# Moving one parameter row, its exponential and the early loads in an S5 + MLP kernel

## The chip, the cores and the metric

One core of one Trainium2 chip. The metric is the device time of one execution in microseconds (us); the medians below are over the timed executions. An execution counts as slow when it is over 1.5% above the fastest of its kernel. All but the slow ones named below had a granted TensorE clock of 1.00 (0.998 and above), with one exception that is also named. One timed execution of each kernel is also the profiled one, from which the lines come; its span, from the first to the last instruction, is nearly 2 us shorter than its time. Spans are compared with spans and timed medians with timed medians.

## The reference, cut to what matters

Two branches read the same 2048 tokens of 640 features; a sigmoid of a dot product mixes them.

```python
# A: a diagonal complex state space model, 640 states
dt      = exp(log_dt)
Lam_bar = exp(dt * (Lambda_re + 1j * Lambda_im))   # |Lam_bar| = exp(dt*Lambda_re) = r_c in the kernel
B_bar   = ((Lam_bar - 1) / Lam)[:, None] * Bmat
h_t     = Lam_bar * h_{t-1} + x_t @ B_bar          # 2048 steps
a       = 2 * real(h @ C) + x * Dskip
# B: an MLP, 640 -> 1728 -> 640
b       = gelu(x @ w1 + b1) @ w2 + b2
out     = g * a + (1 - g) * b,   g = sigmoid(x . gate_w)
```

The kernel turns the complex recurrence into two real scans with the constant factor `r_c`, on inputs rotated by tables of cosine and sine (`TCOS`, `TSIN`). The modulus `r_c` is needed at the first scan; its angle, dt times `Lambda_im`, is needed for the tables.

## The kernel before: the parts concerned

The tokens are handled in four chunks of 512. TensorE, VectorE and ScalarE follow a hand-written order. The early loads go out on two queues, SyncE's and ScalarE's, in the order of this code:

```python
load_x0(nc.sync, 0, 1, 0, KA * P)      # token tile 0, columns 0..255, 64 KB
load_w1a(nc.scalar, 0)                 # slab 0 of w1, 192 KB
load_x0(nc.sync, 1, 2, 0, KA * P)
load_w1a(nc.scalar, 1)
load_x0(nc.sync, 2, 3, 0, KA * P)
load_w1a(nc.scalar, 2)
load_x0(nc.sync, 3, 4, 0, KA * P)
# ... memsets of prmA, prmB ...
nc.scalar.activation(out=warm[:], ..., func=ACT.Exp)        # brings the table in
load_turned(0)                                              # transposed load, columns 256..639
rows(nc.sync,   prmA[2 * KS:3 * KS, :], A_Lambda_re)        # parameter rows, 1.2 KB each
rows(nc.scalar, prmA[0:KS, :], A_log_dt)
rows(nc.scalar, prmA[KS:2 * KS, :], A_Lambda_im)
load_turned(H)
load_w1a(nc.sync, 4)
load_w1a(nc.sync, 3)
# ... w1b slabs; with the second of them the rows of prmB: b1, gate_w ...
```

A row holds one parameter vector as 5 partitions of 128 values. A matmul with an identity turns a tile of rows into columns (`colA`, `colB`), which VectorE and ScalarE can use as scalars:

```python
part(0, 2); part(1, 2); part(0, 3)                          # matmuls of w1 slabs 0 and 1
nc.tensor.matmul(pP[:, 0:3 * KS], lhsT=prmA[:], rhs=ident[:, 0:3 * KS], ...)
nc.vector.tensor_copy(out=colA[:], in_=pP[:, 0:3 * KS])     # log_dt, Lambda_im, Lambda_re
nc.scalar.activation(out=dt16[:], in_=ldt_c, func=ACT.Exp)
# ... limp ...
nc.vector.tensor_tensor(out=dtl[:], in0=dt16[:], in1=lre_c, op=ALU.mult)
nc.vector.tensor_tensor(out=thp_c[:], in0=dt16[:], in1=limp[:], op=ALU.mult)
nc.scalar.activation(out=r_c[:], in_=dtl[:], func=ACT.Exp)
# ... the angles u ...
part(1, 3)
strip(2, 0, HT, False)                                      # first matmuls of w1 slab 2
# ... slabs 2 and 4; the two sines on ScalarE ...
for kf in range(FA):                                        # slab 3
    if kf == 3:
        nc.tensor.matmul(pA[:, 0:NB], lhsT=prmB[:], rhs=ident[:, 0:NB], ...)
        nc.vector.tensor_copy(out=colB[:], in_=pA[:, 0:NB])
# ... GELUs; VectorE widens the sine table by angle doubling ...
nc.vector.tensor_scalar(out=nsH[:], in0=sH, scalar1=-1.0, ...)   # then TCOS, TSIN, then the scans
```

## Time and profile before

| | before |
|---|---|
| time, median of 3 runs, us | 216.03 (215.61 to 216.46) |
| span of the profiled execution, us | 214.29 |
| start of the `colA` copy (VectorE), us | 8.42 |
| start of the `colB` copy (VectorE), us | 12.05 |
| start of the first product of the first scan, us | 28.20 |

The last three rows are the moments by which the start is followed here. The `colA` copy tells when the rows are in, the `colB` copy when VectorE's unbroken work begins, and the first product when the tables are ready. Lines from the queues of ScalarE and SyncE in the timeline (start, length in us, engine, line, operation, output and input):

```profile
0.73 1.39 ACTq L127 DMA_DIRECT2D w1a<-in_B_w_dram  x3
4.04 0.52 ACTq L130 DMA_DIRECT2D prmA<-in_A_log_dt_dram  x1
2.60 1.32 SPq L151 DMA_TRANSPOSE xT<-in_A_x_dram  x1
```

Slab 2 is the third of the first line and goes out at about 1.65. The rows go out only at 4.04, and the first transposed load at 2.60.

### The profile page before, as it was taken

What the parts mean: (1) busy time and instruction counts of PE and PEld (TensorE: products, weight loads), DVE (VectorE), ACT (ScalarE), POOL (GpSimd) and SP (SyncE); (2) the same over time, 40 slices, a digit from 0 to 9 for tenths busy, and PEclk for the clock granted to TensorE, in tenths of its full rate; (3) what the DMA queues carried; (4) which work ended last, traced back from release to release, by engine and by line L of the source; (5) the groups of instructions that cost most, each with busy time, mean ns of one, the idle gap of its engine ahead of it and who ended that gap; (6) DMA issues with size and microseconds to landing.
All of it is one profiled execution on the core that took longest, in us unless ns stands there. A gap on an engine that the chain in (4) does not pass through costs nothing.

```text
span 214.3 us, 3539 instructions
## 1 busy us (share of the span) xinstructions
PE 209.6 (98%) x1383; PEld 125.6 (59%) x1383; DVE 187.9 (88%) x381; ACT 101.7 (47%) x182; POOL 1.9 (1%) x15
## 2 busy tenths in 40 slices
PE   8899999999999999999999999999999999999994
PEld 5745444454576644775457777444457577676773
DVE  2489999999998999998999999899999999995153
ACT  3499856675759579203663210456682421405100
POOL 1001000000000000000000000000000000000000
DMA  6899999999000000051000005100000000110012
GB/s 183 207 177 206 206 202 286 348 195 227 3 0 0 3 0 0 14 173 50 25 0 3 0 0 177 45 26 0 2 5 12 0 3 0 61 64 0 0 63 64
DMA packets 33139, 16.23 MB, mean 76 GB/s; under 512 B 24546, under 2 KB 33122, under 8 KB 33122
## 3 DMA queue, kind: packets, MB, share of 16 engines
q1 hardware_dynamic: 32526, 15.38, 29.9%
q10 hardware_dynamic: 596, 0.63, 0.9%
q8 instruction: 11, 0.18, 0.4%
q14 instruction: 6, 0.05, 0.1%
HBM read 7.48 MB, written 2.62 MB: 47 GB/s over the span
## 4 chain that ended last, share of the span: by engine, by line
DVE 70%; PE 20%; DMA 5%; issue 2%; ACT 1%; ACTq 0%; DVEq 0%
DVE g L497 19%; PE bank L661 10%; DVE wa L478 10%; DVE wb L478 10%; PE bank L602 7%; DVE v L478 6%; DVE hs L478 6%; DMA out_dram<-ot 4%; DVE bank L576 3%; DVE ot L666 3%; PE bank L274 2%; DMA prmA<-in_A_Lambda_im_dram 2%; DVE CT_re L466 2%; DVE CT_im L466 2%; DVE g L426 1%
## 5 line engine op out<-in xcount | busy, mean ns | idle before, releaser
L602 PE MATMUL bank<-w_sb,gel 128*128 128x384 bf16 (+1 forms) x416 | 57.9, 299 | 0.0
L602 PEld LDWEIGHTS <-gel 128*128 128x128 bf16 x416 | 40.3, 98 | 17.0 <-issue 0.8
L546 ACT ACTIVATE bu<-bank 128x512 bf16<-128x512 f32 x40 | 23.6, 597 | 37.3 <-PE bank L543 37.2
L661 PEld LDWEIGHTS <-hs 128*128 128x128 bf16 x330 | 31.7, 98 | 12.1 <-issue 0.4
L279 ACT ACTIVATE gel<-bank,colB 128x512 bf16<-128x512 f32 x52 | 33.7, 694 | 10.6 <-PE bank L274 10.3
L497 DVE TENSOR_TENSOR_SCAN g<-r_c,carry,v 128x512 bf16<-128x512 f32 x30 | 37.2, 1270 | 0.0
L610 ACT ACTIVATE gb<-bank,gcol 128x384 f32<-128x384 f32 (+1 forms) x32 | 15.1, 526 | 31.7 <-PE bank L602 16.5
L274 PE MATMUL bank<-xT,w1a 128*128 128x512 bf16 (+2 forms) x162 | 27.7, 328 | 0.0
L666 DVE SCALAR_TENSOR_TENSOR ot<-bank,gcol,gb 128x320 bf16<-128x320 f32 (+2 forms) x33 | 17.5, 532 | 11.5 <-PE bank L661 9.5
L661 PE MATMUL bank<-CT_re,hs 128*128 128x320 bf16 (+2 forms) x165 | 27.1, 295 | 0.2 <-DVE bank L576 0.2
L661 PE MATMUL bank<-CT_im,hs 128*128 128x320 bf16 (+2 forms) x165 | 27.1, 295 | 0.0
L543 PE MATMUL bank<-xT,BT_re 128*128 128x512 bf16 x100 | 24.9, 379 | 0.0
L543 PE MATMUL bank<-xT,BT_im 128*128 128x512 bf16 x100 | 24.8, 379 | 0.0
L274 PEld LDWEIGHTS <-w1a 128*128 128x128 bf16 x162 | 14.4, 101 | 11.7
L274 PE MATMUL bank<-xT,w1b 128*128 128x512 bf16 x80 | 17.9, 379 | 0.0
L543 PEld LDWEIGHTS <-BT_im 128*128 128x128 bf16 x100 | 9.8, 98 | 11.8
L591 ACT ACTIVATE bank<-b2bc 128x384 f32<-128x384 bf16 (+1 forms) x24 | 11.7, 530 | 9.3 <-DVE ot L666 9.3
L543 PEld LDWEIGHTS <-BT_re 128*128 128x128 bf16 x100 | 9.7, 98 | 11.0
L478 DVE TENSOR_TENSOR v<-wa,wb 128x512 bf16<-128x512 bf16 x40 | 15.2, 421 | 0.6
L576 DVE TENSOR_TENSOR bank<-xn,Dbc 128x320 f32<-128x320 bf16 (+2 forms) x33 | 14.3, 481 | 1.0 <-ACT gb L610 0.9
L478 DVE TENSOR_TENSOR wa<-TCOS,g 128x1024 bf16<-128x1024 bf16 x20 | 13.7, 685 | 0.1
L478 DVE TENSOR_TENSOR wa<-TCOS,bu 128x1024 bf16<-128x1024 bf16 x20 | 13.7, 684 | 0.0
(103 smaller groups left out, 168.1 us busy)
## 6 DMA issues: line engine op xcount, KB each, us to landing
out_dram<-ot SPq DMA_DIRECT2D x15, 160.0 KB, 1.9
w_sb<-in_B_w_dram SPq DMA_DIRECT2D x1, 2080.0 KB
xn<-in_A_x_dram SPq DMA_DIRECT2D x2, 640.0 KB, 4.2
w1b<-in_B_w_dram SPq DMA_DIRECT2D x5, 128.0 KB, 2.9
xn<-in_A_x_dram SPq DMA_DIRECT2D x2, 320.0 KB, 3.1
w1a<-in_B_w_dram ACTq DMA_DIRECT2D x3, 192.0 KB, 3.9
w1a<-in_B_w_dram SPq DMA_DIRECT2D x2, 192.0 KB, 3.1
xn<-in_A_x_dram SPq DMA_DIRECT2D x1, 384.0 KB
```

What stands on the lines that cost most here:

```text
L274: nc.tensor.matmul(p[:, t0:t1], lhsT=w, rhs=xT[c][:, kd, t0:t1], start=(kd == 0) if first is None else first, stop=(kd == last), skip_grou ...
L279: nc.scalar.activation(out=gel[c][:, kf, :], in_=p[:, :], func=ACT.Gelu_apprx_tanh, bias=b1_c[:, kf:kf + 1])
L478: nc.vector.tensor_tensor(out=o, in0=a, in1=b, op=op)
L497: nc.vector.tensor_tensor_scan(s["g"][:, ri, :], r_c[:, ks:ks + 1].to_broadcast([P, CH]), s["v"][:, ri, :], init, ALU.mult, ALU.add)
L543: nc.tensor.matmul(p[:], lhsT=BT[ks >= KSA][:, kd, (ks % KSA if ks < KSA else ks - KSA) * P:][:, 0:P], rhs=xT[c][:, kd, :], start=(kd == 0 ...
L546: nc.scalar.activation(out=bu[:, ri, :], in_=p[:], func=ACT.Identity)
L576: dve_now(ck.pe, 0.45, lambda: nc.vector.tensor_tensor(out=p[:, 0:d1 - d0], in0=xn[c][:, a, d0:d1], in1=Dbc[:, d0:d1], op=ALU.mult))
L591: nc.scalar.activation(out=v, in_=src, func=ACT.Identity)
L602: nc.tensor.matmul(p[:, col:col + d1 - d0], lhsT=gel[c][:, kf, a * P:(a + 1) * P], rhs=w2_sb[:, kf, d0:d1], start=False, stop=False, skip_ ...
L610: nc.scalar.activation(out=gbs[ti][:, d0:d1], in_=p[:, col:col + d1 - d0], func=ACT.Identity, scale=gcol[:, 1, ti:ti + 1])
L661: nc.tensor.matmul(p[:, 0:d1 - d0], lhsT=hs[c][:, j, lo:lo + P], rhs=CT[:, j % KS, d0:d1], start=False, stop=(j == 2 * KS - 1), skip_group ...
L666: nc.vector.scalar_tensor_tensor(out=ot[:, d0:d1], in0=p[:, 0:d1 - d0], scalar=gcol[:, 0, ti:ti + 1], in1=gbs[ti][:, d0:d1], op0=ALU.mult, ...
```

## The change

The intent: the angle of the tables does not need `Lambda_re`, so that row leaves the early group and travels with the bias rows. The modulus then cannot be exponentiated early, and a late Exp was expected to cost two table loads between the GELUs; it is computed as exp(z) = (1 + tanh(z/2)) / (1 - tanh(z/2)), as Tanh runs beside GELU with no load. The two remaining rows are issued sooner, and the transpose that needs them is moved forward. Two token loads become one, and slab 2 goes behind the transposed loads.

```diff
-    load_x0(nc.sync, 2, 3, 0, KA * P)
-    load_w1a(nc.scalar, 2)
-    load_x0(nc.sync, 3, 4, 0, KA * P)
+    load_x0(nc.sync, 2, 4, 0, KA * P)
 ... (memsets)
+    rows(nc.scalar, prmA[0:KS, :], A_log_dt)
+    rows(nc.scalar, prmA[KS:2 * KS, :], A_Lambda_im)
 ... (warm activation)
     load_turned(0)
-    rows(nc.sync, prmA[2 * KS:3 * KS, :], A_Lambda_re)
-    rows(nc.scalar, prmA[0:KS, :], A_log_dt)
-    rows(nc.scalar, prmA[KS:2 * KS, :], A_Lambda_im)
     load_turned(H)
+    load_w1a(nc.scalar, 2)
 ... (after b1 and gate_w)
+            rows(nc.sync, prmB[NB:NB + KS, :], A_Lambda_re)
 ... (the prmA matmul, colA copy, dt16, limp, thp_c, u: from behind part(0, 3) to before part(1, 2);
      without the product dtl and the Exp of r_c)
-            nc.tensor.matmul(pA[:, 0:NB], lhsT=prmB[:], ...)
-            nc.vector.tensor_copy(out=colB[:], in_=pA[:, 0:NB])
+            nc.tensor.matmul(pA[:, 0:NB + KS], lhsT=prmB[:], ...)
+            nc.vector.tensor_copy(out=colB[:], in_=pA[:, 0:NB + KS])
+            nc.vector.tensor_tensor(out=dtl[:], in0=dt16[:], in1=lre_c, op=ALU.mult)
 ... (after the first GELUs)
+    nc.scalar.activation(out=thr[:], in_=dtl[:], func=ACT.Tanh, scale=0.5)
 ... (before the widening of the table)
+    nc.vector.tensor_scalar(out=rden[:], in0=thr[:], scalar1=-1.0, scalar2=1.0, ...)   # 1 - t
+    nc.vector.reciprocal(out=rden[:], in_=rden[:])
+    nc.vector.tensor_scalar(out=thr[:], in0=thr[:], scalar1=1.0, ...)                  # 1 + t
+    nc.vector.tensor_tensor(out=r_c[:], in0=thr[:], in1=rden[:], op=ALU.mult)
     nc.vector.tensor_scalar(out=nsH[:], in0=sH, scalar1=-1.0, ...)
```

The load of the second chunk's tokens is also split in two halves, late in the queue.

More of the change, by code (lines that the diff above doesn't have):

```diff
@@ L98 @@
     prmB = const.tile([P, P], BF16, name="prmB")
-    colA = const.tile([P, 3 * KS], F32, name="colA")
-    colB = const.tile([P, NB], F32, name="colB")
+    colA = const.tile([P, 2 * KS], F32, name="colA")
+    colB = const.tile([P, NB + KS], F32, name="colB")
     Dbc = const.tile([P, D], BF16, name="Dbc")
@@ L115 @@
     lim_c = colA[:, KS:2 * KS]
-    lre_c = colA[:, 2 * KS:3 * KS]
+    lre_c = colB[:, NB:NB + KS]
     b1_c = colB[:, KS:NB]
@@ L192 @@
     nc.sync.dma_start_transpose(out=xT[3][:], in_=x2d[3 * CH:4 * CH, :])
-    load_xn(1)
+    load_xn(1, 0, H)
+    load_xn(1, H, TPC)
     ctx.enter_context(tc.manual_schedule(engines={E.PE, E.DVE, E.Activation}))
@@ L267 @@
     r_c = col("r_c")
+    thr = col("thr")
     hs = [None] * NCH
@@ L368 @@
     part(0, 2)
+    pP = bank()
+    nc.tensor.matmul(pP[:, 0:2 * KS], lhsT=prmA[:], rhs=ident[:, 0:2 * KS], start=True, stop=True, skip_group_check=True)
+    nc.vector.tensor_copy(out=colA[:], in_=pP[:, 0:2 * KS])
+    nc.scalar.activation(out=dt16[:], in_=ldt_c, func=ACT.Exp)
+    nc.vector.tensor_scalar(out=limp[:], in0=lim_c, scalar1=INV_2PI, scalar2=None, op0=ALU.mult)
+    nc.vector.tensor_tensor(out=thp_c[:], in0=dt16[:], in1=limp[:], op=ALU.mult)
+    nc.vector.tensor_tensor(out=u, in0=tf[:].rearrange("p (o i) -> p o i", o=1).to_broadcast([P, KS, NP]), in1=over(thp_c[:], NP), op=ALU.mult)
     part(1, 2)
     part(0, 3)
-    pP = bank()
-    nc.tensor.matmul(pP[:, 0:3 * KS], lhsT=prmA[:], rhs=ident[:, 0:3 * KS], start=True, stop=True, skip_group_check=True)
-    nc.vector.tensor_copy(out=colA[:], in_=pP[:, 0:3 * KS])
-    nc.scalar.activation(out=dt16[:], in_=ldt_c, func=ACT.Exp)
-    nc.vector.tensor_scalar(out=limp[:], in0=lim_c, scalar1=INV_2PI, scalar2=None, op0=ALU.mult)
-    nc.vector.tensor_tensor(out=dtl[:], in0=dt16[:], in1=lre_c, op=ALU.mult)
-    nc.vector.tensor_tensor(out=thp_c[:], in0=dt16[:], in1=limp[:], op=ALU.mult)
-    nc.scalar.activation(out=r_c[:], in_=dtl[:], func=ACT.Exp)
-    nc.vector.tensor_tensor(out=u, in0=tf[:].rearrange("p (o i) -> p o i", o=1).to_broadcast([P, KS, NP]), in1=over(thp_c[:], NP), op=ALU.mult)
     part(1, 3)
@@ L390 @@
         if kf == 3:
-            nc.tensor.matmul(pA[:, 0:NB], lhsT=prmB[:], rhs=ident[:, 0:NB], start=True, stop=True, skip_group_check=True)
-            nc.vector.tensor_copy(out=colB[:], in_=pA[:, 0:NB])
+            nc.tensor.matmul(pA[:, 0:NB + KS], lhsT=prmB[:], rhs=ident[:, 0:NB + KS], start=True, stop=True, skip_group_check=True)
+            nc.vector.tensor_copy(out=colB[:], in_=pA[:, 0:NB + KS])
+            nc.vector.tensor_tensor(out=dtl[:], in0=dt16[:], in1=lre_c, op=ALU.mult)
         ff1_mm(banks[kf], 0, kf, 3, 0, CH, False, 3)
@@ L401 @@
         ff1_act(two_banks[i], 0, FA + i)
+    nc.scalar.activation(out=thr[:], in_=dtl[:], func=ACT.Tanh, scale=0.5)
+    act(0.2)
     for t, k0, k1 in ((w1c_lo, 0, 3), (w1c_hi, 3, KD)):
@@ L421 @@
     nsH = col("nsH")
+    rden = col("rden")
+    nc.vector.tensor_scalar(out=rden[:], in0=thr[:], scalar1=-1.0, scalar2=1.0, op0=ALU.mult, op1=ALU.add)
+    nc.vector.reciprocal(out=rden[:], in_=rden[:])
+    nc.vector.tensor_scalar(out=thr[:], in0=thr[:], scalar1=1.0, scalar2=None, op0=ALU.add)
+    nc.vector.tensor_tensor(out=r_c[:], in0=thr[:], in1=rden[:], op=ALU.mult)
     nc.vector.tensor_scalar(out=nsH[:], in0=sH, scalar1=-1.0, scalar2=None, op0=ALU.mult)
```

## The prediction

> **What bounds the kernel now.** I read the busy shares of the page first, then the waits of TensorE, then the chain that ended last in order of time, then the timeline of each engine in the first 30 us.
>
> ```profile
> PE 209.6 (98%) x1383; PEld 125.6 (59%) x1383; DVE 187.9 (88%) x381; ACT 101.7 (47%) x182; POOL 1.9 (1%) x15
> ...
> DVE 70%; PE 20%; DMA 5%; issue 2%; ACT 1%; ACTq 0%; DVEq 0%
> ```
>
> The two lines seem to disagree: TensorE is busy 98% of 214.3 us, yet 70% of the chain that ended last is VectorE. Both are nearly full, so the question is which of the two a saving must shorten. The waits of TensorE answer it:
>
> ```profile
> PE bank L372 <- DMA prmA<-in_A_Lambda_im_dram: 0.9, 1, 0.9
> PE bank L237 <- PEq L720: 0.8, 1, 0.8
> PE bank L661 <- DVE bank L576: 0.2, 1, 0.2
> ```
>
> TensorE waits three times in the whole run: 0.78 us at the start, 0.88 us at 7.33 us for the parameter rows (the wait that the change attacks), and 0.24 us near 174.4 us, where the third output stage waits for VectorE to seed its bank. The last one is short, but it decides. Around it the chain of waits reads:
>
> ```profile
> 4.60 3.47 DMA prmA<-in_A_Lambda_im_dram
> 8.38 3.60 PE bank L274 x27
> 12.05 0.18 DVE colB L392
> 12.23 0.09 DVE sq L418
> 12.33 0.09 DVE cq L418
> 12.44 0.49 DVE gel L410
> ...
> 19.40 0.83 DVE hs L415
> 20.34 0.36 DVE g L426
> ...
> 174.18 0.42 DVE bank L576
> 174.65 11.09 PE bank L661 x80
> ```
>
> From 12.05 to 174.60 the chain is VectorE's own work with short detours: one ScalarE fold at 63.6 us and two output transfers (from 94.8 and 131.8 us), each released by VectorE itself. None of its waits in this stretch is on a matmul. So whatever shifts VectorE at 12 us shifts the seed at 174.6 us by the same amount, and from there TensorE runs through to 211.5 us. TensorE alone, if it came sooner, would only wait longer at 174.4. Any gain must therefore arrive through VectorE, and its start hangs on the small copy at 12.05, which waits for a matmul in TensorE's order:
>
> ```profile
> 8.21 0.17 PE L372 MATMUL bank<-ident,prmA 128*128 128x15 bf16 x1 [0.88 <-DMA prmA<-in_A_Lambda_im_dram]
> 8.42 0.17 DVE L373 COPY colA<-bank 128x15 f32<-128x15 f32 x1 [1.82 <-PE bank L372]
> 11.25 0.58 ACT L388 ACTIVATE hs<-gel,halfpi 128x345 f32<-128x345 f32 x1
> 12.05 0.18 DVE L392 COPY colB<-bank 128x18 f32<-128x18 f32 x1 [0.83 <-PE bank L391]
> ```
>
> The second sine ended at 11.83, so two things became ready almost together there: the sines and the second parameter transpose (L391, at 11.82 in TensorE's order).
>
> **What the Trainium skill says.** "ScalarE activation tables: per-element evaluation and per-set limits", opening section: two functions in one table set need no switch, in different sets they are one load of 1283 ns apart. The trace agrees: each load takes 1.28 us, and the Tanh of the gate runs straight after a GELU at 21.25 us with no load, so the new tanh costs none. "ScalarE: Activation LUTs", section "What ACT_TABLE_LOAD costs", gives a switch 2.66 us with its drain; here the load at 9.29 is followed by its sine at 10.70, a distance of 1.41 us, and I use that. "VectorE: DVE Perf Modes", section "Rules for kernel authors", advises to minimize the count of operations rather than the semaphores. Four more operations on the chain are the wrong direction by that rule; the trace gives their price below. "DMA: Bandwidth & Descriptors", section "Anatomy of one DMA", fits about 2.0 us of fixed cost per transfer for the GpSimd path; here, under load, a row of 1.2 KB on the hardware queue took 3.47 us, so issue time and queueing matter more than size.
>
> **The change part by part.**
>
> *Rows sooner.* Both rows on ScalarE's queue move ahead of the table load and the warm activation. They were issued at 4.04 and 4.60; behind two weight loads (0.73 plus twice 0.46) they go at about 1.65 and 2.15. The second landed 3.47 us after issue, so about 5.6 now. The matmul that needs them moves six matmuls forward, to about 6.5. It should not wait, and the gap of 0.88 us closes: everything of TensorE behind 7.33 can come 0.88 us earlier. The trigonometry starts at about 6.7 instead of 8.42, and the second sine should end near 9.9, so the sines no longer hold VectorE at all. It then waits for L391, at 11.82 - 0.88 = 10.94.
>
> *Transposes sooner.* The queue of SyncE is issue-bound from 0.73 to 11.6 us. One token load less saves 0.42 us, the Lambda row 0.49: the first transposed load goes at about 2.15 (was 2.60), the second at 3.5 (was 4.53), the later weights about 0.7 sooner once the Lambda row is issued among the bias rows. This mostly keeps pace with a TensorE that comes 0.88 us earlier; it does not pay by itself. Against it, the third weight slab of w1a goes from about 1.7 to about 4.3 us on ScalarE's queue. Loads of its kind took 3.0 to 3.9 us, so it lands at 7.3 to 8.2; it will be wanted at about 7.7. The transfer engines are saturated there (share 0.93 to 1.11 in each microsecond from 3 to 8), so I charge 0 to 0.5 us.
>
> *Lambda with the biases.* The product of dt and Lambda can be formed only after the second parameter copy. It now stands between that copy and the copies of sine and cosine. Dependent small operations of this kernel start 0.20 us apart (34.98, 35.18, 35.38), independent ones 0.08. Before, 0.39 us passed from the copy to the first product (12.05 to 12.44); now the copy, 0.20, the product, 0.08, 0.08 and 0.21: 0.57. Cost 0.18 us, on the path.
>
> *Exponential through tanh.* One ScalarE exponential (0.21 us) goes, at a place where it delayed the sine's table; a tanh of about 0.17 comes among the GELUs, with ScalarE far ahead of VectorE's need: nothing on the path. But VectorE gets four small operations just before the table is widened: the denominator, its reciprocal 0.20 later, the numerator about 0.10 after that, the product 0.20 after that, and the old negation 0.08 behind. That is 0.58 us more from 20.14 on, on the path, as VectorE has no idle time there.
>
> *Sum.* At the first scan VectorE gains 0.88 from TensorE and loses 0.18 + 0.58 = 0.76: a net gain of 0.12 us. The early token loads without the third slab beside them may add up to 0.3; a wait for that slab may take up to 0.5. About 0.15 us is my central gain. The split of the second chunk's token load (issued at 48.4, landing 4.2 us later, first read at 121.6) buys or costs nothing.
>
> **The rivals.** *TensorE sets the end.* Then closing the gap gives 0.88, with the 0.24 perhaps 1.1 us: about 215.0. For it speaks the 98%; against it the wait at 174.4, which grows as TensorE comes sooner and VectorE does not. *A new wait takes the old one's place.* If the third slab lands at 8.2, half of the gain goes; if the new row behind the bias rows is late, L391 waits: it is issued at about 7.15, and with the 3.5 to 4.1 us of the earlier rows it would land at 10.7 to 11.3, against 10.94. Either turns the sum into a loss of 0.2 to 0.4 us: about 216.4. For it speaks the saturation to 8 us; against it that the share falls to 0.62 in the microsecond from 9, where the new row travels. *Later transfers fall behind.* The last weight slabs landed at about 16.1 and 16.7 and are read at 16.6 and 17.2; if they do not move with the rest, TensorE loses 0.3 us, but behind VectorE's start, and it costs nothing at the end. *A tighter seed elsewhere.* With TensorE 0.76 us nearer to VectorE, the first bank of the second output stage, seeded by 122.15 and read at 123.06, has about 0.1 us left: a possible small wait, free as well, since VectorE is not moved by it.
>
> **Range and chances.** 216.03 - 0.15 = 215.9 us. The repeats of the kernel before spread from 215.61 to 216.46, and the rivals sit at 215.0 and 216.4. A range of 215.1 to 216.6 holds it 8 times in 10, tilted neither way by much. A change of 2% would be 4.3 us; nothing here is that large: 1% faster, 98% within 2%, 1% slower.
>
> **What would show each step.** The wait for the rows is gone from TensorE's waits, and the colA copy starts near 6.7. The colB copy starts near 11.1 (was 12.05); later than 11.6 means a new wait. Four small operations of 0.16 to 0.19 us stand before the negation, and the first product of the first scan begins near 28.1 (was 28.20). TensorE's wait for the seed near 174 us grows from 0.24 to about 1 us, at that bank or at an earlier seed. If that wait is instead gone and the span is a microsecond shorter, I had the wrong engine.

## More of the kernel before

The finished output tile comes from a pool of two: `ot = fwork.tile([P, D], BF16, name="ot", bufs=2)`. After each tile SyncE stores it.

## The result, and the profile after

| | before | after |
|---|---|---|
| time, median of 6 fast runs, us | 215.87 (215.59 to 216.46) | 217.94 (216.87 to 218.65) |
| span of the profiled execution, us | 214.29 | 215.01 |
| `colA` copy, us | 8.42 | 7.48 |
| `colB` copy, us | 12.05 | 12.06 |
| first product of the first scan, us | 28.20 | 28.97 |
| from there to the end, us | 186.09 | 186.04 |

The ratio of the fast runs is 1.0089, 95% interval 1.0059 to 1.0118. Ratios in this document are the mean time of one kernel's fast runs over that of the other's of the same rounds, so not quite the ratio of the medians quoted. The changed kernel is slower by nearly 2 us, within 2%, but outside the predicted range: the sign was wrong.

The last row of the table says where to look. From the first product to the end both kernels take the same 186 us; the loss of this trace, 0.72 us of span, lies in the first 29 us. The traced execution is the fastest of the six (216.87 against a median of 217.94), so this trace shows only part of the loss. VectorE's timeline there:

```profile
12.06 0.18 DVE L391 COPY colB<-bank 128x23 f32<-128x23 f32 x1 [1.82 <-PE bank L390]
12.28 0.17 DVE L392 TENSOR_TENSOR dtl<-dt,colB 128x5 f32<-128x5 bf16 x1
...
20.36 0.17 DVE L425 TENSOR_SCALAR rden<-thr 128x5 f32<-128x5 f32 x1
20.56 0.19 DVE L426 RECIPROCAL rden<-rden 128x5 f32<-128x5 f32 x1
20.66 0.13 DVE L427 TENSOR_SCALAR thr<-thr 128x5 f32<-128x5 f32 x1
20.83 0.17 DVE L428 TENSOR_TENSOR r_c<-thr,rden 128x5 f32<-128x5 f32 x1
20.91 0.17 DVE L429 TENSOR_SCALAR nsH<-sq 128x5 f32<-128x5 f32 x1
```

The added operations stand where they were foreseen, and `nsH` comes 0.55 us behind `rden`. What was not foreseen is the first line: `colB` starts at 12.06, as before, though the rows no longer held TensorE. All the waits of TensorE (total, count, longest, in us) confirm that the old wait has gone, and that the seed wait near 174 us has grown:

```profile
PE bank L668 <- DVE bank L583: 0.8, 1, 0.8
PE bank L237 <- PEq L727: 0.8, 1, 0.8
```

The chain of waits for the first 13 us (start, length in us, what) names what took the place of the rows:

```profile
0.74 0.41 ACTq L127
...
1.17 3.26 DMA w1a<-in_B_w_dram
...
4.45 4.07 DMA w1a<-in_B_w_dram
...
8.56 1.48 PE bank L275 x12
...
12.06 0.19 DVE colB L391
```

Slab 1 (issued at 1.17) lands at 4.43; at once ScalarE's queue issues slab 2, at 4.45; it lands at 8.52, and TensorE's matmuls with it begin at 8.56. In this trace TensorE's weight loads were idle only 0.27 us for it, because TensorE itself was late (it reached full rate at 6.40 us, against 5.11 before: the moment from which some 20 matmuls of 128 columns start in a microsecond and not 10 or 11).

The two queues, to be set beside the three lines of before:

```profile
1.67 0.57 ACTq L130 DMA_DIRECT2D prmA<-in_A_log_dt_dram  x1
4.45 0.36 ACTq L127 DMA_DIRECT2D w1a<-in_B_w_dram  x1
2.13 2.65 SPq L151 DMA_TRANSPOSE xT<-in_A_x_dram  x2
```

Rows and transposes are sooner by 2.37 and 0.47 us, and slab 2 later by 2.8 us.

### The profile page after: what moved, and what is told of

Same layout as the page of the kernel before. It is cut to its first block, busy times and chain, and to the rows that moved or that the text cites. A ratio compares the mean times of both kernels' runs of the same rounds, so it can differ in the third digit from the quotient of the medians.

```text
span 215.0 us, 3533 instructions
## 1 busy us (share of the span) xinstructions
PE 210.0 (98%) x1372; PEld 126.1 (59%) x1383; DVE 188.8 (88%) x385; ACT 101.4 (47%) x182; POOL 2.6 (1%) x15
## 3 DMA queue, kind: packets, MB, share of 16 engines
HBM read 7.48 MB, written 2.62 MB: 47 GB/s over the span
## 4 chain that ended last, share of the span: by engine, by line
DVE 70%; PE 19%; DMA 7%; issue 2%; ACT 1%; ACTq 0%; DVEq 0%
DVE g L504 19%; PE bank L668 10%; DVE wa L485 10%; DVE wb L485 10%; PE bank L609 7%; DVE v L485 6%; DVE hs L485 6%; DMA out_dram<-ot 4%; DMA w1a<-in_B_w_dram 3%; DVE bank L583 3%; DVE ot L673 3%; PE bank L275 2%; DVE CT_re L473 2%; DVE CT_im L473 2%; DVE g L433 1%
## 5 line engine op out<-in xcount | busy, mean ns | idle before, releaser
L275 PE MATMUL bank<-xT,w1a 128*128 128x512 bf16 (+2 forms) x158 | 28.2, 333 | 0.3
L485 DVE TENSOR_TENSOR wb<-TSIN,g 128x1024 bf16<-128x1024 bf16 x20 | 13.7, 686 | 0.0
```

Of the source, the lines that this page charges most:

```text
L275: nc.tensor.matmul(p[:, t0:t1], lhsT=w, rhs=xT[c][:, kd, t0:t1], start=(kd == 0) if first is None else first, stop=(kd == last), skip_grou ...
L485: nc.vector.tensor_tensor(out=o, in0=a, in1=b, op=op)
```

## The experiments

**The theories.** The slab theory: slab 2, issued late among the transposed loads, is what TensorE waits for; the start gains nothing, the tanh form costs its 0.76 us, and the sum is a loss. Rivals: the start was only unlucky in this one trace (TensorE's slow first microseconds fell longer); the tanh form costs more than 0.76; the loss lies later, at the output transfers. Fifteen runs were made, in four groups, each group on one chip beside the kernel before; the first two groups share that chip and 11 executions of the kernel before. The first eight sort the parts; the next three test the rows without disturbing the slabs and look at the kernel before a second time; the last four look at the changed kernel again and take the output waits away. All the kernels gave the correct result.

Timed results, us (median of the kernel before beside them: 215.76 for the first four rows, 215.73 for the next four, 215.72 for the two `g_` rows, 215.89 for the last two):

| run | what it is | median (lowest to highest) | ratio, 95% |
|---|---|---|---|
| a_again | changed kernel | 217.52 (217.21 to 220.06) | 1.0106, 1.0070 to 1.0143 |
| a_w1a2_third | changed, slab 2 early again | 216.92 (216.69 to 217.47) | 1.0061, 1.0043 to 1.0079 |
| b_tanh | before + tanh form | 216.26 (215.69 to 216.96) | 1.0031, 1.0009 to 1.0054 |
| c_rows_first | before + rows sooner | 216.40 (216.05 to 216.67) | 1.0031, 1.0014 to 1.0049 |
| a_pool | changed, modulus on GpSimd | 217.00 (215.69 to 219.26) | 1.0036, 1.0009 to 1.0064 |
| a_loads_undone | changed, old tokens and slab | 216.92 (216.35 to 219.76) | 1.0052, 1.0031 to 1.0074 |
| p_pool | b_tanh, modulus on GpSimd | 215.64 (215.41 to 216.06) | 1.0003, 0.9986 to 1.0020 |
| a_split | changed, token loads apart | 216.82 (216.62 to 217.24) | 1.0056, 1.0039 to 1.0073 |
| g_rows | changed rows from GpSimd's queue | 216.94 (216.25 to 219.74) | 1.0055, 1.0031 to 1.0079 |
| g_pool | g_rows, modulus on GpSimd | 215.90 (215.68 to 216.20) | 1.0010, 0.9991 to 1.0030 |
| a_ot3 | changed, three output tiles | 216.44 (215.88 to 216.91) | 1.0020, 1.0004 to 1.0037 |
| b_ot3 | before, three output tiles | 215.39 (215.05 to 216.01) | 0.9983, 0.9969 to 0.9998 |

One execution each of a_pool (219.26), a_loads_undone (219.76) and g_rows (219.74) is slow, at a clock of 0.991 or 0.992. These three are left out of the ratios, but not of the medians; without them the medians are 217.00, 216.91 and 216.72. The 220.06 of a_again, also at 0.992, is 1.3% above the fastest, so it counts as fast and is in the ratio; without it the ratio of the means would be 1.0087, close to the 1.0089 of the result. `before_again` (215.57), `a_look2` (217.40) and `a_look3` (218.53) are one look each.

The moments in the traces, us. The sixth column is the distance from `colB` to the first product, the price of what VectorE does between them; the last is from the first product to the end:

| trace | colA | colB | first product | span | colB to product | product to end |
|---|---|---|---|---|---|---|
| before | 8.42 | 12.05 | 28.20 | 214.29 | 16.15 | 186.09 |
| before_again | 7.63 | 11.27 | 27.40 | 213.66 | 16.13 | 186.26 |
| after | 7.48 | 12.06 | 28.97 | 215.01 | 16.91 | 186.04 |
| a_again | 7.01 | 12.44 | 29.34 | 215.51 | 16.90 | 186.17 |
| a_look2 | 6.56 | 11.81 | 28.71 | 215.63 | 16.90 | 186.92 |
| a_look3 | 6.89 | 12.81 | 29.70 | 216.75 | 16.89 | 187.05 |
| a_w1a2_third | 7.95 | 12.26 | 29.16 | 215.33 | 16.90 | 186.17 |
| b_tanh | 7.82 | 11.43 | 28.34 | 214.40 | 16.91 | 186.06 |
| c_rows_first | 7.88 | 12.19 | 28.32 | 214.89 | 16.13 | 186.57 |
| a_pool | 6.87 | 12.66 | 28.83 | 215.22 | 16.17 | 186.39 |
| a_loads_undone | 7.23 | 11.84 | 28.74 | 215.16 | 16.90 | 186.42 |
| p_pool | 8.31 | 11.95 | 28.12 | 213.88 | 16.17 | 185.76 |
| a_split | 7.35 | 11.66 | 28.56 | 214.88 | 16.90 | 186.32 |
| g_rows | 6.84 | 11.15 | 28.04 | 215.75 | 16.89 | 187.71 |
| g_pool | 7.41 | 11.72 | 27.87 | 214.42 | 16.15 | 186.55 |
| a_ot3 | 7.38 | 12.58 | 29.48 | 214.45 | 16.90 | 184.97 |
| b_ot3 | 7.89 | 11.53 | 27.68 | 213.28 | 16.15 | 185.60 |

The sixth column takes two values only, whatever else changes: 16.13 to 16.17 without the tanh operations on VectorE, 16.89 to 16.91 with them.

### a_again: the changed kernel once more

No edit.

> The changed kernel unaltered, to see what of its first trace repeats. In that trace TensorE ran at half rate until 6.4 us (before: 5.1), waited for the third w1a slab until 8.56, and VectorE's second parameter copy (colB) started at 12.06, as before the change. Theory 'slab': the wait for the slab near 8.5 and colB at 12.0 to 12.3 are there again, time near 217.9. Theory 'clock': the moment of full rate is a matter of chance, lies elsewhere between 4 and 8 us, and colB and the time go with it (colB 11.4 to 12.8, time 216.5 to 218.7).

Measured: 217.52 us, so the loss repeats. In the trace TensorE's slow phase ended early (full rate at 5.43 us), and the wait for slab 2 stands open, in TensorE's timeline:

```profile
8.95 3.43 PE L275 MATMUL bank<-xT,w1a 128*128 128x256 bf16 x20 [0.95 <-DMA w1a<-in_B_w_dram]
```

TensorE was through with its earlier work at 8.0 and stood 0.95 us. With a faster TensorE only the wait is longer and `colB` is not earlier: this speaks for the slab and against the unlucky start.

### a_w1a2_third: slab 2 early again

```diff
     load_w1a(nc.scalar, 1)
+    load_w1a(nc.scalar, 2)
     load_x0(nc.sync, 2, 4, 0, KA * P)
 ...
     load_turned(H)
-    load_w1a(nc.scalar, 2)
```

> The changed kernel with the third w1a slab issued third on ScalarE's queue again, ahead of the two rows. Theory 'slab': no wait for w1a any more, colB at 11.0 to 11.6, time 0.5 to 1.0 us below the changed kernel (about 217.1). Theory 'clock': TensorE arrives no sooner unless full rate does, time within 0.3 us of the changed kernel.

Measured: 216.92 us, ratio 1.0061. The slab wait is gone, but `colB` stands at 12.26. TensorE's timeline shows a new first wait:

```profile
6.35 0.28 PE L240 MATMUL bank<-ident,xn 128*128 128x128 bf16 x2 [1.43 <-DMA xn<-in_A_x_dram]
```

The merged token load, now behind three slabs, landed at 6.31, and TensorE waited 1.43 us for it. So the slab's late place in the change pays for the merged load's early landing (5.29 in the first trace of the changed kernel). Putting the slab back alone does not restore the start: `colB` misses the 11.0 to 11.6 expected. The time is nevertheless about 0.6 us below the changed kernel's, as expected, and this trace does not explain that.

### b_tanh: the tanh form alone

The kernel before, with `Lambda_re` in `prmB` and `colB`, the product behind the `colB` copy, the tanh and the four small operations. The order of slabs, tokens and the other two rows is that of before.

```diff
-    rows(nc.sync, prmA[2 * KS:3 * KS, :], A_Lambda_re)
 ...
+            rows(nc.sync, prmB[NB:NB + KS, :], A_Lambda_re)
 ... (dtl, thr, rden, r_c as in the change)
```

> The kernel before with only Lambda's move to the bias rows and the tanh form of the exponential. If my price of these operations is right, colB stays at 12.05, the first product of the first scan starts at 28.95 (before 28.20), TensorE's wait for the seed near 174 us grows to about 1.0, and the time is 0.75 us above before (about 216.65). The rival that VectorE has hidden slack: time equal to before within 0.2 us.

Measured: 216.26 us, ratio 1.0031, a loss of 0.67 us (0.0031 of 215.8), and 16.91 us from `colB` to the first product against 16.15. The tanh form costs what was worked out, 0.76 us in the trace, and not more, so the rival of a dearer tanh falls. So does that of hidden slack. `colB` came at 11.43, not at 12.05: with one row fewer `log_dt` went out at 3.23 instead of 4.04, and TensorE did not wait for the rows.

### c_rows_first: the rows alone

The kernel before, with its exponential; the three rows on ScalarE's queue behind the three slabs, ahead of the warm activation, and the transpose of the rows before part(1, 2).

```diff
+    rows(nc.scalar, prmA[0:KS, :], A_log_dt)
+    rows(nc.scalar, prmA[KS:2 * KS, :], A_Lambda_im)
+    rows(nc.scalar, prmA[2 * KS:3 * KS, :], A_Lambda_re)
     warm = ...
     load_turned(0)
-    rows(nc.sync, prmA[2 * KS:3 * KS, :], A_Lambda_re)
-    rows(nc.scalar, prmA[0:KS, :], A_log_dt)
-    rows(nc.scalar, prmA[KS:2 * KS, :], A_Lambda_im)
```

> The kernel before with only the three parameter rows issued ahead of the table load on ScalarE's queue (behind all three slabs) and their matmul six matmuls sooner; the exponential stays. If VectorE's start sets the end: no wait for the rows, colB near 11.2, first product of the first scan near 27.3, time 0.6 to 0.9 us below before (about 215.2). If the clock's late release takes the gain: colB at 11.6 to 12.1 and the time within 0.3 us of before.

Measured: 216.40 us, ratio 1.0031. This run shows that sooner rows alone, without a late slab, do not gain here; they lose. Its trace has no wait for rows, and `colB` at 12.19. SyncE's queue and ScalarE's timeline show what paid:

```profile
3.75 2.65 SPq L154 DMA_TRANSPOSE xT<-in_A_x_dram  x2
...
4.63 1.28 ACT L151 ACT_TABLE_LOAD   x1 [4.63 <-DVE xT L247]
```

The transposed loads went out at 3.75 (2.60 before). ScalarE came to its table load only at 4.63 (2.15 before) and so was late with a copy that TensorE waited 0.4 us for. The chain of waits runs this way in full: slab 1 lands at 4.32, the third row goes out at 4.34, then come the table load, the copy, TensorE at 6.35 and `colB`.

**What holds the transposed loads back** is visible if the issue time of the first of them is set beside its place in the order in which the trace has SyncE and ScalarE issue their transfers. As the seventh it went out at 2.13 (after), as the eighth at 2.60 (before, b_tanh), as the ninth at 3.38 (a_split), as the tenth at 3.85 (a_loads_undone) and 3.75 (c_rows_first). In the trace the landings of these transfers are counted on eight semaphores. A ninth transfer reuses the semaphore of an early one, and its issue waits until that one has landed. In the last three runs the first transposed load waits for slab 0 and goes out 0.02 us after its landing. SyncE's waits in c_rows_first name it:

```profile
SPq L154 <- DMA w1a<-in_B_w_dram: 1.2, 1, 1.2
```

In the changed kernel slab 2, the tenth transfer, reuses the semaphore of slab 1 and goes out 0.02 us after slab 1 has landed, in all seven traces in which it has this place (a_split is the seventh). No run changed the number of semaphores; but in g_rows, where the rows land on two others, the first transposed load goes out at 2.59.

### a_pool: the modulus on GpSimd, in the changed kernel

The product and a fourth-order series with two squarings run on GpSimd; the tanh and VectorE's four operations go.

```diff
-            nc.vector.tensor_tensor(out=dtl[:], in0=dt16[:], in1=lre_c, op=ALU.mult)
+            nc.gpsimd.tensor_tensor(out=dtl[:], in0=dt16[:], in1=lre_c, op=ALU.mult)
-    nc.scalar.activation(out=thr[:], in_=dtl[:], func=ACT.Tanh, scale=0.5)
+    ... ten nc.gpsimd operations of 128x5 that give r_c ...
-    ... rden, reciprocal, thr + 1, r_c on VectorE ...
```

> The changed kernel with its transfers and its order on TensorE untouched, but r = exp(dt times Lambda) formed on GpSimd by a short series (dtl too), so VectorE is free of the five small operations and ScalarE of the tanh. If these cost 0.76 us on the path that sets the end: from the colB copy to the first product of the first scan 16.15 us again (changed kernel 16.91), and the time 0.75 us under the changed kernel (217.6), about 216.85, still above before by 1. Rival: the small operations are not what the time is made of: time within 0.2 us of the changed kernel.

Measured: median 217.00 us, ratio 1.0036: 0.0053 less than the changed kernel's 1.0089 and 0.0070 less than a_again's 1.0106 (0.0051 without its 220.06), with wide intervals. The trace shows 16.17 us from `colB` to the first product. But `colB` itself stands at 12.66, with 1.30 us of wait for slab 2. The price of the tanh form and the slab are two separate losses: taking one away leaves the other.

### a_loads_undone: old tokens and slab, new rows

```diff
-    load_x0(nc.sync, 2, 4, 0, KA * P)
+    load_x0(nc.sync, 2, 3, 0, KA * P)
+    load_w1a(nc.scalar, 2)
+    load_x0(nc.sync, 3, 4, 0, KA * P)
 ...
-    load_w1a(nc.scalar, 2)
```

> The changed kernel with the token loads apart and the third slab third on ScalarE's queue, as before the change; rows ahead of the table load, early matmul, Lambda with the biases and the tanh stay. Theory 'order of transfers' (the loss beyond 0.76 comes from the slab issued late and from the merged token load landing late): no wait for the slab or tokens, colB at 11.2 to 11.6, time 215.9 to 216.4, at or below the tanh alone (216.26). Rival (a new transfer is issued only after an earlier one of the eight counters has landed, so the rows that go early hold back the transposed loads behind them): the transposed loads are issued at 3.3 us or later, TensorE waits for them, colB at 12 or later, time 216.9 or more.

Measured: 216.92 us, ratio 1.0052. `colB` is at 11.84. The waits of TensorE have spread. The largest falls at 14.89 us, behind `colB`, and so does not delay VectorE's start:

```profile
PE bank L276 <- DMA w1b<-in_B_w_dram: 0.7, 1, 0.7
```

Ahead of `colB` come 0.4 us for a slab of w1a, 0.3 us for a copy of ScalarE and 0.2 us for a token tile.

The slabs waited for stand behind the transposed loads on SyncE's queue, which itself was held until 3.85. The rival's issue time and total time came true; TensorE's waits, though, were not for the transposed loads themselves. The ratio is 0.004 to 0.005 below the full change and the kernel still behind the kernel before.

### p_pool: no tanh on VectorE, loads as before

b_tanh with the series on GpSimd, as in a_pool.

> The kernel before with only Lambda's move to the bias rows, r formed on GpSimd. In the run with the tanh alone the rows landed by 7.3 (before 8.1), TensorE did not wait for them and colB started at 11.4, but VectorE then lost 0.76. Without that loss the first product of the first scan starts at 27.5 to 27.8 and the time is 0.3 to 0.7 us below before: about 215.3, better than both kernels. If GpSimd is too slow, the first scan waits for r_c beyond 30.2 us.

Measured: 215.64 us, ratio 1.0003. That is 0.6 us below b_tanh (1.0003 and 1.0031 of 215.8), and the distance from `colB` to the first product is 16.17. With both losses out, the time of before is back, but nothing is gained: TensorE waited 0.53 us for the rows here, `colB` stands at 11.95 and the first product at 28.12, not at 27.5 to 27.8.

### a_split: only the token loads apart

```diff
-    load_x0(nc.sync, 2, 4, 0, KA * P)
+    load_x0(nc.sync, 2, 3, 0, KA * P)
+    load_x0(nc.sync, 3, 4, 0, KA * P)
```

> The changed kernel with only the merged token load taken apart again; the third slab stays late. If the merge costs: the third token tile is there 0.3 us or more sooner, and the time is 0.3 us or more below the changed kernel. If the slab alone sets TensorE's arrival: the wait for the slab stays (1 us or more), time within 0.3 us of the changed kernel (217.6), or above, as one more transfer stands ahead of the slab.

Measured: 216.82 us, ratio 1.0056. The slab stayed late (issued at 4.26), but with the transposed loads issued only at 3.38 there was no wait for it in this trace: `colB` 11.66. The slabs of this trace, this one included, were in flight for 3.1 to 3.3 us, so the same slab at the same issue time is about a microsecond or more faster when only one transposed load goes out ahead of it (at 3.38) and not two (in the changed kernel at 2.13 and 3.52). Of the orders with the rows early on ScalarE's queue this is the earliest `colB`, and the total still is the price of the tanh form plus a little. Both signs of the first alternative came: the third token tile landed at 4.70 (the merged load at 4.82 to 5.36), and the time is 0.7 us or more lower. But the wait that went was the one for the slab, so this does not show that the merge itself costs.

### before_again: the kernel before, a second look

No edit.

> The kernel before once more, for a second trace: over the ten traces so far the span was the start of the first product of the first scan plus 185.8 to 186.6 us. Here too: colB between 11.4 and 12.1, the product 16.15 later, the span 186.1 after that. The moment of TensorE's full rate may lie anywhere from 4.2 to 6.5 us without moving colB much, as the wait for the rows follows it.

Measured: 215.57 us. The trace corrects the prediction's starting point:

```profile
7.43 0.17 PE L372 MATMUL bank<-ident,prmA 128*128 128x15 bf16 x1
7.45 3.75 PE L274 MATMUL bank<-xT,w1a 128*128 128x128 bf16 x27
```

The matmul that needs the rows has no wait in front of it at all, and `colB` stands at 11.27, earlier than expected. So much of the 0.88 us that the change set out to save was a property of one execution. With the other traces whose loads are those of before, save for one row (b_tanh, p_pool, b_ot3), the wait for the rows was 0.88, 0, 0, 0.53 and 0.25: 0.33 us in the mean.

### g_rows: the rows from a queue that disturbs nobody

The loads of before; `log_dt` and `Lambda_im` issued by GpSimd behind the identity; the rest as in the change.

```diff
-    rows(nc.scalar, prmA[0:KS, :], A_log_dt)
-    rows(nc.scalar, prmA[KS:2 * KS, :], A_Lambda_im)
 ...
     make_identity(nc, ident[:])
+    rows(nc.gpsimd, prmA[0:KS, :], A_log_dt)
+    rows(nc.gpsimd, prmA[KS:2 * KS, :], A_Lambda_im)
```

> The change's idea without its cost in transfers: the loads of before (tokens apart, slab third), log dt and Lambda's imaginary part issued from GpSimd's queue, their matmul six matmuls sooner, Lambda's real part with the biases, the tanh form on VectorE. If the loss beyond the tanh comes from putting the rows into the queue and the counters ahead of the loads: no wait for slab, tokens or rows, transposes at 2.6 us, colB at 10.9 to 11.3, first product of the first scan near 27.9 (16.91 later), time 215.2 to 215.8, that is 2 us under the changed kernel. If the saturated transfers bound the start in any order: TensorE waits somewhere before 10 us and colB is 11.6 or later, time 216.3 or more.

Measured: 216.94 us, ratio 1.0055. Its trace shows the start that was predicted for the change: the rows are issued at 1.47, there is no wait for them, `colA` at 6.84, `colB` at 11.15 and the first product at 28.04 (28.1 predicted). The span is nevertheless 215.75, because the rest took 187.71 us instead of 186. A line of VectorE's waits says why:

```profile
DVE ot L673 <- DMA out_dram<-ot: 3.3, 2, 2.3
```

VectorE waited 3.3 us in two waits for a free output tile (1.8 in the first trace of before), as one store took 5.68 us, and passed the delay to TensorE, which waited 2.4 us for the seed. That is one trace, and it is of the slowest of the five fast executions (217.53). The other four, 216.25 to 217.16, are above the expected 215.2 to 215.8 as well, and no trace says why. Why the store was slow stays open too.

### g_pool: the same with the modulus on GpSimd

> The same, with r formed on GpSimd by the series instead of the tanh form on VectorE: colB at 10.9 to 11.3, first product 16.15 later, at 27.1 to 27.5, time 0.6 to 1.0 us below before (about 214.9), better than both kernels. If the start is bound by the saturated transfers: colB 11.6 or later and no gain over before beyond 0.3 us.

Measured: 215.90 us, ratio 1.0010. The difference to g_rows is 0.0045, or 1.0 us, of which 0.74 us is the tanh form (16.89 against 16.15). Its trace again differs at the start, with 0.63 us of wait for the fourth token tile and `colB` at 11.72. It is not faster than before, as its second alternative said.

### a_look2 and a_look3: the changed kernel, two more looks

No edit.

> The changed kernel, another trace. Its traces so far put colB at 12.06 and 12.44 (12.66 with the same transfers in a_pool), which with 0.76 for the tanh explains some 1.5 of the 1.8 to 2.2 us that the timed runs lose; its timed runs are mostly slower than its traced ones. If the start is the whole cause: colB 12.4 to 13.5 here when the run is slow, and span minus the first product still 186.0 to 186.4. If the rest is lost later: colB near 12.4, but span minus first product above 186.5.

> As a_look2, a further trace: same alternatives, colB 12.4 to 13.5 and a tail of 186.0 to 186.4, or colB near 12.4 and a longer tail.

Measured: 217.40 and 218.53 us; TensorE waited 0.77 and 1.44 us for slab 2. The second look's timeline and chain:

```profile
9.31 3.43 PE L275 MATMUL bank<-xT,w1a 128*128 128x256 bf16 x20 [1.44 <-DMA w1a<-in_B_w_dram]
```

```profile
4.29 4.97 DMA w1a<-in_B_w_dram
...
12.81 0.19 DVE colB L391
```

Slab 2 was in flight for 4.97 us here, and one store from 133.45 took 5.06 us. Both looks also show 2.6 and 2.7 us of output waits on VectorE, where before and before_again have 1.8 and 2.0 (0.8 of the latter is put down to TensorE in the list of waits, but the chain of waits shows the store). From the first product to the end they take 186.92 and 187.05 us, so part of the loss lies behind the start. The full rate of TensorE came at 4.00 and 4.46 us in these two, earlier than in the profile of before (5.11): the rival of the unlucky start falls for good.

### a_ot3 and b_ot3: three output tiles

```diff
-            ot = fwork.tile([P, D], BF16, name="ot", bufs=2)
+            ot = fwork.tile([P, D], BF16, name="ot", bufs=3)
```

the first in the changed kernel, the second in the kernel before.

> The changed kernel with three output tiles instead of two. VectorE waits for an output transfer twice (near 98 and 136 us, 1.7 to 1.9 us in all), in the stretch in which VectorE alone sets the end. If VectorE is the bound until 174 us, taking these waits away gives TensorE's wait for the seed (0.8 to 1.0 us) back: that wait gone or below 0.2, the tail 185.1 to 185.4 instead of 186.1, time 0.7 to 1.0 us below the changed kernel (217.6), near 216.7, although nothing at the start is touched. If the end hangs on TensorE or on the start alone: no more than 0.2 us.

> The kernel before with three output tiles. TensorE waits there only 0.24 to 0.4 us for the seed, so with the output waits gone no more than that comes back: 215.3 to 215.6, against 215.73. If the output transfers also cause part of the spread, the runs lie closer together. Below 215.0 would mean that VectorE holds TensorE somewhere that I have not seen.

Measured: 216.44 and 215.39 us. VectorE's wait for a free output tile is gone in both, and so is TensorE's wait for the seed near 174 us. All the waits of TensorE in the changed kernel with three tiles:

```profile
PE bank L237 <- PEq L727: 0.8, 1, 0.8
PE bank L275 <- DMA w1a<-in_B_w_dram: 0.7, 1, 0.7
```

Now TensorE sets the end, and the tanh form, VectorE's burden, should cost nothing. What remains between the two kernels is TensorE's start: the ratios differ by 0.0037, or 0.8 us, and the `colB` copies by 12.58 - 11.53 = 1.05 us. This isolates the loss of the start in timed runs. The third tile takes 1.1 to 1.5 us from the changed kernel (216.44 against 217.52 and 217.94) and about 0.4 from the kernel before, where TensorE is only that far from being the bound: its seed waits were 0.24 and 0.4 us. The kernel before with three output tiles is the fastest measured, by a small margin (interval 0.9969 to 0.9998).

## Why the prediction was wrong

**Which engine sets the end: right.** The span follows the first product by 186.0 to 186.6 us in 11 of the 15 traces with two output tiles, through differences of two microseconds at the start. TensorE's wait for the seed grew from 0.24 to 0.8, 1.0, 1.7 and 1.8 us in the four traces of the changed kernel; about 1 us was foretold, and the last two have the longer output waits in them.

**The price of Lambda with the biases and of the tanh: right.** 0.18 + 0.58 = 0.76 us was predicted; 16.91 - 16.15 = 0.76 was measured in the trace, and 0.6 to 0.7 us in the timed runs of b_tanh, and of p_pool against it.

**Rows sooner: the issue times right, the gain wrong. This is the step that failed.** The prediction said that "the gap of 0.88 us closes: everything of TensorE behind 7.33 can come 0.88 us earlier", and it charged "0 to 0.5 us" for the third slab. Both terms were mis-sized. The wait for the rows, taken from one profile, was 0.33 us in the mean of five traces. And the slab was issued about when predicted (4.3), at 4.27 to 4.45, but was in flight for 3.97 to 4.97 us in the six traces with the change's loads (after, a_again, a_look2, a_look3, a_pool, a_ot3), not the 3.0 to 3.9 of "loads of its kind", and landed at 8.27 to 9.26, not at "7.3 to 8.2". TensorE stood 0.27 to 1.44 us for it in these six, 0.91 in the mean (in `after` this is the idle time of its weight loads, in the others of its matmuls). The landing sets the start: in all six `colB` begins 3.54 or 3.55 us after it, whether TensorE came to its full rate at 4.00 us or at 6.40. So the rival "a new wait takes the old one's place" was the right one, at about twice the size given to it.

As a sum over the traces: `colB` stood at 11.65 in the mean of the five with the loads of before (before, before_again, b_tanh, p_pool, b_ot3), and at 12.39 in the mean of the six with the change's. The start is 0.74 us later where 0.88 less 0 to 0.5 was to be gained. The two waits account for 0.91 - 0.33 = 0.58 of it. Added to 0.76 this is 1.5 us of the 1.8 to 2.1 us between the medians (217.52 against 215.76, 217.94 against 215.87).

**Why the slab was slow** is shown in part. The prediction knew that the transfer engines are busy in this time, but the three slabs whose landing its trace shows were issued at 1.67, 5.79 and 6.42, none of them near 4.4. The windows of the changed kernel, microsecond by microsecond (last two columns: share of time in which the transfer engines are busy, and GB/s):

```profile
3.00:4.00 1.00, 1.00 (x10) 0.78 (x9) 0.34 (x2) 0.99 (x2) 0.00 (x0) 1.00 1.09 360
4.00:5.00 1.00, 1.00 (x11) 0.95 (x10) 0.44 (x2) 0.24 (x2) 0.00 (x0) 1.00 0.96 199
5.00:6.00 1.00, 1.00 (x13) 1.00 (x11) 0.20 (x1) 0.23 (x2) 0.00 (x0) 1.00 0.93 136
6.00:7.00 1.00, 1.00 (x17) 1.00 (x16) 0.16 (x2) 0.20 (x2) 0.00 (x0) 1.00 0.95 156
7.00:8.00 1.00, 1.00 (x20) 0.89 (x17) 0.60 (x4) 0.56 (x3) 0.00 (x0) 1.00 1.05 317
```

While the two transposed loads are on their way, the engines are as busy as before but move 136 to 199 GB/s, against 360 and 317 on either side. Slab 2 falls into just this valley. That the transposes make the valley is likely; no run separated it. The nearest is a_split, with one of them ahead of the slab and 3.06 us in flight. The order alone is not enough: in before, two slabs issued at 5.79 and 6.42, behind both transposed loads, took 3.14 and 3.00 us.

**What takes the gain in the other orders** is the same budget in other hands. With the token load merged and three slabs ahead of it, it is the tokens (1.43 us). With three rows ahead of the transposed loads, it is ScalarE's table load, which stands behind the last of them. With tokens apart, slab early and rows early, it is several small waits. Only rows from a queue of their own gave the start that was predicted, in one of two traces.

**Later transfers: open.** About 0.4 us of the loss is left for the part behind the first product: 186.55 us in the mean of the four traces of the changed kernel, 186.18 in the two of before. It comes from two of the four, which show output waits of 2.6 and 2.7 us; the other two take 186.04 and 186.17. That points to slower stores in some executions. The runs with three output tiles do not prove it: their larger gain in the changed kernel is about as large as the tanh form's 0.76 us, which a VectorE freed of these waits no longer shows. Why stores are slow in some executions, and whether the change makes them slow more often, is open; the prediction had no such term.

**The merged token load and the split of the second chunk's load.** The first cannot be had alone: it moves the transposed loads forward and, with the slab in its old place, the tokens back. The second was charged with nothing, and no run tested it alone.

## What to carry to other kernels

Before pricing a wait from a profile, look at a second profile of the same kernel: a wait in the first ten microseconds can be half chance (0.88 us here, 0.33 in the mean of five traces). A small load moved ahead is not small in its effects where transfers are issued in a fixed order and the engines that move them are full: ask which load falls back a place, and price that one with durations from the time in which it will travel. And where two engines are within half a microsecond of each other, work put on the later one costs all of its time, and a saving on the earlier one brings nothing; an extra output buffer, which takes a wait from the later one, was the only edit here that gained, about 0.4 us.

## What the Trainium skill lacked or had wrong

- No page has that transfers of such a kernel go out late because of the place that they take in the order of all transfers. Here the first transposed load went out at 2.12 to 2.60 us where it was among the first eight of the two queues. As the ninth or tenth it waited for the landing of slab 0 and went out at 3.38, 3.75 and 3.85. The late slab 2, the tenth, went out 0.02 us after the landing of slab 1.
- "DMA: Bandwidth & Descriptors", section "Anatomy of one DMA", gives about 2.0 us and the bytes at 436 GB/s for one transfer, which makes about 2.5 us for a slab of 192 KB (an estimate from the page). In the six traces with the change's loads slab 0 took 2.77 to 2.95 us, slab 1 3.09 to 3.26 us and the one issued behind the transposed loads 3.97 to 4.97 us; in `after` the engines were then busy 0.93 to 0.96 of the time and moved 136 to 199 GB/s. The page says of its fit that it is for another path than the one these slabs took, and it has none for transfers under load.
- "TensorE: Matmul & The Clock Gate", in the part on what one observes of the clock gate, puts the change to the full rate at around 4 us of sustained activity, plus or minus 500 ns from run to run. Here the first matmul ran at about 0.78 us and the full rate came between 3.99 and 6.40 us in 17 traces, 3.2 to 5.6 us after it: a wider spread. The granted clock shows 1.00 all the while.
